# Attention, a Mish MLP and a SoLU MLP on one core: the SoLU MLP's first product computed for pairs of token tiles by a seven-product scheme

## The chip, the cores and the metric

The kernel runs on one core of a Trainium2 chip. The metric is the device time of one execution in microseconds, smaller being better. Engines are named as in the profile: PE (TensorE, matmuls; PEld its weight loads), DVE (VectorE), ACT (ScalarE), POOL (GpSimd), SP (SyncE, which issues the DMAs here).

## The reference

Causal attention over a window of 64 (4 x 8 heads, 576 tokens, head size 64) feeds an MLP with the Mish function (512 to 2048 to 512), and that feeds a second MLP, with SoLU and a LayerNorm (512 to 1024 to 512). There are 2304 tokens.

```python
x = attention(q, k, v)                      # 2304 x 512
h = x @ w_in                                # first MLP, 2048 wide
x = (h * np.tanh(log1p(exp(h)))) @ w_out
h = x @ w_in2                               # second MLP, 1024 wide: the change is here
e = np.exp(h - max(h))
solu = h * (e / (sum(e) + 1e-09))
mu = mean(solu);  var = mean((solu - mu) ** 2)
ln = (solu - mu) / np.sqrt(var + 1e-06) * g_ln
return ln @ w_out2
```

## The kernel before

**Number format.** Every fp32 product is made of three matmul terms: each operand is split in a high part rounded to a short format (`round_12`) and a rest (`rest`), and high x rest, high x high and rest x high are summed in PSUM. The weights arrive as 64-bit numbers; four steps on ACT and DVE (`c_up`, `c_low`, `c_bits`, `c_sign`, lines 350 to 372) turn a piece of them in a staging buffer `st` into fp32, and `c_hi`, `c_lo` split it into a weight buffer (`w1` or `w2` ring, four buffers each). g_ln is multiplied into the last weights in the same split.

**First MLP.** Tokens stand in groups of 512, 512, 512, 384 and 384. An item is one group by one block of 128 hidden units; there are 84. Item i has 12 matmuls into `ps_h` (`pe_m1`, L742), Mish on ACT and DVE, and 12 more into the four output banks `x_0` to `x_3` (`pe_m2`, L776, and `pe_m2l`, L787). Attention (lines 462 to 727) is computed in pieces between the items of the first groups. A group's output is copied out by L812 and L814 and stored to a scratch tensor `x2d`.

**Second MLP.** It goes by tiles of 128 tokens, t = 0 to 17. `b_load` fetches a tile into `xr`; `b_split` (ACT, L855) and `b_rest` (POOL, L860) split it into `xs`; `b_m3` (L870) makes 24 matmuls of 128 x 512 into the two banks of `h2`, turn by turn: four blocks of the contraction by three terms by two halves of the 1024 columns. Then comes a chain of one tile: `b_max` (DVE, L877), `b_exp` with a row sum (ACT, L883), `b_stat` (DVE: product with h in L889, two `bn_stats` in L892, L894 to L899), `b_var` (POOL, L904 and L905, the inverse square root by `pow`), `b_z` (DVE, L910 and L911), eight transposes on PE (`b_tr`, L918), the split of the transposed tile (`b_hi` on ACT, L924; `b_lo` on DVE, L928), 24 matmuls into one bank `po` (`b_m4`, L943), `b_out` (ACT, L950) and the store. `h2` has two buffers, one for even and one for odd tiles.

**Order.** Nothing is ordered by hand. Every piece of work is a `step` with its costs on the engines that may do it, a due time and the steps it has to come after. `Schedule.run` (line 113) takes, again and again, the step that can start first by its own planned costs, and among those that can start within `PATIENCE` the one that is due first. Buffers are rings (`w1=4, w2=4, st=2, ...`): a step that needs a new one waits until the users of the oldest are done. The due times of every stage come from number tables (`MISH_AT`, `ATT_AT`, `PRE_AT`, `B_AT`, `CONV_PRIO`, ...), so one number in a table can move instructions on all engines. In each engine's queue the instructions are then executed in the order that results.

**Where PE has nothing to do** in the first stage, small bf16 matmuls on a zero tile (L516) are put in; 42 of them stand at the start.

Of the kernel before, what the change touches and what calls it, by code (L numbers as in the profile page):

```python
# [24 lines left out]
P = 128  # L25
# [30 lines left out]
B_AT = (9.587, 37.912, -19.559, -30.209, 0.809, 34.651, 64.819, 43.703)

CONV_PRIO = (43.465, 59.161, 15.699, 11.465, 9.993, -9.387)
Q_LEAD = 1.101
V_LEAD = -62.18  # L60
G_AT = 1.058
K0_LATER = -88.806
FIRST_AT = (-161.938, -95.173, -8.712)
W_STEP = 0.88
M4_LATER = -28.799
BESIDE_AT = ((12.83, 25.285), (5.132, 29.901), (-14.786, 53.657), (-18.384, 60.677), (13.158, 1.338))
BESIDE_PE = 15.387
PATIENCE = 0.35
SLACK = 7.152
# [6 lines left out]
N_STAGED = 4  # L76
W1_PIECES = ((0, 1), (1, 1), *((f, 2) for f in range(2, 16, 2)))
# [119 lines left out]
def attention_moe_solu(  # L197
# [81 lines left out]
    tctx = ExitStack()  # L279
    ld_p = tctx.enter_context(tc.tile_pool(name="ld", bufs=LD, side="right"))  # L280
# [541 lines left out]
    with tc.manual_schedule():  # L822
# [8 lines left out]

        def open_b():
            tctx.close()
            B["x"] = ctx.enter_context(tc.tile_pool(name="bx", bufs=2, side="right", reuse_waits="tile"))
            B["s"] = ctx.enter_context(tc.tile_pool(name="bs", bufs=4, side="right", reuse_waits="tile"))
            B["h0"] = ctx.enter_context(tc.tile_pool(name="pb_h0", bufs=1, space=PSUM, side="right", reuse_waits="tile"))
            B["mhalf"] = B["s"].tile([P, 1], F32, name="mhalf", bufs=1)
            nc.vector.memset(B["mhalf"], -0.5)

        def open_b2():  # L840
# [4 lines left out]
            B["h1"] = ctx.enter_context(tc.tile_pool(name="pb_h1", bufs=1, space=PSUM, reuse_waits="tile"))  # L845

        def b_load(t):
            j, o = tile_of[t]
            xr[t] = B["x"].tile([P, KD, P], F32, tag="xr", name="xr", bufs=1)
            nc.sync.dma_start(out=xr[t], in_=x2d[j][:, :, o:o + P])  # L850

        def b_split(t):
            r = xr.pop(t)
            xs[t] = B["x"].tile([P, 2, KD, P], F32R, tag="xs", name="xs", bufs=2)
            nc.scalar.activation(out=xs[t][:, 0], in_=r, func=ACTF.Copy)  # L855
            xr[t] = r

        def b_rest(t):
            r = xr.pop(t)
            nc.gpsimd.tensor_tensor(out=xs[t][:, 1], in0=r, in1=xs[t][:, 0].bitcast(F32), op=ALU.subtract)  # L860

        def b_m3(t):
            h2[t] = B["h" + str(t % 2)].tile([P, 2, 512], F32, tag="h2", name="h2")
            x = xs.pop(t)
            assert all(("w3", c, k) in split_done for c in range(2) for k in range(KD))

            terms = [(k, a, b) for k in range(KD) for a, b in ((0, 1), (0, 0), (1, 0))]
            for idx, (k, a, b) in enumerate(terms):
                for c in range(2):
                    nc.tensor.matmul(  # L870
                        out=h2[t][:, c, :], lhsT=x[:, a, k, :], rhs=wt["w3", c][:, b, k, :],
                        start=(idx == 0), stop=(idx == len(terms) - 1),
                    )

        def b_max(t):
            nm = B["s"].tile([P, 1], F32, tag="nm", name="nm")
            nc.vector.tensor_reduce(out=nm, in_=h2[t], axis=AX.XY, op=ALU.max, negate=True)  # L877
            nrm[t] = nm

        def b_exp(t):  # L880
            y = B["x"].tile([P, 2, 512], F32, tag="y", name="y")
            su = B["s"].tile([P, 1], F32, tag="su", name="su")
            nc.scalar.activation(out=y, in_=h2[t], func=ACTF.Exp, bias=nrm[t], accum_out=su)  # L883
            nrm[t] = y, su

# [371 lines left out]
```

## Time and profile before

| | us |
|---|---|
| median of 3 runs | 705.45 (704.46 to 706.88) |
| profiled execution | 706.97 |
| its span, first to last instruction | 705.1 |
| PE busy | 695.4 (4429 matmuls) |
| DVE busy | 382.0 |
| ACT busy | 312.1 |
| POOL busy | 56.9 |

Busy time is the sum over an engine's instructions. Matmuls are pipelined and overlap in the profile's bars, so one matmul's listed duration is longer than the time that it adds to the span; what one adds is read from the chain of waits, where consecutive matmuls of one line form a piece with its length and count.

### The profile page before, as it was taken

What the parts mean: (1) busy time and instruction counts of PE and PEld (TensorE: products, weight loads), DVE (VectorE), ACT (ScalarE), POOL (GpSimd) and SP (SyncE); (2) the same over time, 40 slices, a digit from 0 to 9 for tenths busy, and PEclk for the clock granted to TensorE, in tenths of its full rate; (3) what the DMA queues carried; (4) which work ended last, traced back from release to release, by engine and by line L of the source; (5) the groups of instructions that cost most, each with busy time, mean ns of one, the idle gap of its engine ahead of it and who ended that gap; (6) DMA issues with size and microseconds to landing.
All of it is one profiled execution on the core that took longest, in us unless ns stands there. A gap on an engine that the chain in (4) does not pass through costs nothing.

```text
span 705.1 us, 10722 instructions
## 1 busy us (share of the span) xinstructions
PE 695.4 (99%) x4429; PEld 597.2 (85%) x4429; DVE 382.0 (54%) x559; ACT 312.1 (44%) x536; POOL 56.9 (8%) x80
## 2 busy tenths in 40 slices
PE   9989999999999999999999999999999999999997
PEld 7779888888888888878899999999888888888886
DVE  4988776775662121656614114666766556565550
ACT  5769977475442222454534325663322222222231
POOL 2111000010000000000001100001122212111000
PEclk9999999999999999999999999999999999999999
DMA  8747355846213030323150105330111111110011
GB/s 288 296 156 293 121 178 179 278 160 219 90 46 106 0 119 31 119 91 120 31 165 1 31 1 165 120 119 32 44 59 46 46 45 46 46 45 31 16 45 46
DMA packets 37856, 71.74 MB, mean 102 GB/s; under 512 B 2864, under 2 KB 15152, under 8 KB 37808
## 3 DMA queue, kind: packets, MB, share of 16 engines
q1 hardware_dynamic: 37808, 71.06, 29.9%
q8 instruction: 35, 0.57, 0.3%
q14 instruction: 13, 0.11, 0.0%
HBM read 59.51 MB, written 11.53 MB: 101 GB/s over the span
## 4 chain that ended last, share of the span: by engine, by line
PE 94%; DVE 3%; DMA 2%; ACT 1%; issue 0%; SPq 0%; ACTq 0%
PE ps_h L742 27%; PE x L776 18%; PE h L870 14%; PE po L943 14%; PE x L787 9%; PE ps_o L696 2%; PE pt L918 2%; PE ps_t L659 2%; PE ps_s L564 2%; PE ps_w L516 1%; DMA st<-w_in 1%; DMA room_kv<-v 1%; PE ps_s L546 1%; DVE w L308 0%; DVE g L308 0%; DVE su L633 0%
## 5 line engine op out<-in xcount | busy, mean ns | idle before, releaser
L742 PE MATMUL ps_h<-xt,w 128*128 128x512 f32 (+2 forms) x1008 | 212.3, 361 | 0.3 <-ACT mc L752 0.2
L742 PEld LDWEIGHTS ps_h<-xt,w 128*128 128x128 f32 x1008 | 178.1, 189 | 22.9 <-issue 1.0
L776 PE MATMUL x<-g,w 128*128 128x512 f32 (+2 forms) x672 | 147.9, 362 | 0.0
L776 PEld LDWEIGHTS x<-g,w 128*128 128x128 f32 x672 | 118.1, 188 | 14.6 <-issue 0.9
L308 DVE SCALAR_TENSOR_TENSOR g<-mc,g 128x512 fp32r<-128x512 f32 (+2 forms) x84 | 53.2, 635 | 117.5 <-ACT g L288 117.0
L870 PE MATMUL h<-w,xs 128*128 128x512 f32 x432 | 104.0, 396 | 0.0
L943 PE MATMUL po<-w,lz 128*128 128x512 f32 x432 | 102.8, 394 | 0.0
L870 PEld LDWEIGHTS h<-w,xs 128*128 128x128 f32 x432 | 80.9, 188 | 19.0
L943 PEld LDWEIGHTS po<-w,lz 128*128 128x128 f32 x432 | 80.0, 188 | 16.3
L288 ACT ACTIVATE g<-mc 128x512 fp32r<-128x512 f32 (+2 forms) x70 | 39.8, 572 | 97.9 <-PE x L787 97.5
L787 PE MATMUL x<-g,w 128*128 128x512 f32 (+2 forms) x336 | 81.2, 363 | 0.0
L752 ACT ACTIVATE mc<-ps_h 128x512 f32<-128x512 f32 (+2 forms) x84 | 44.6, 535 | 78.1 <-PE ps_h L742 64.3
L787 PEld LDWEIGHTS x<-g,w 128*128 128x128 f32 x336 | 59.1, 188 | 7.1 <-issue 0.5
L924 ACT ACTIVATE lz<-pt 128x512 fp32r<-128x512 f32 x36 | 19.6, 596 | 63.2 <-PE po L943 49.5
L877 DVE TENSOR_REDUCE nm<-h 128x1 f32<-128x1024 f32 x18 | 22.0, 1224 | 45.8 <-PE h L870 45.8
L647 POOL TENSOR_TENSOR s<-s,rs 128x1024 f32<-128x1024 f32 x7 | 13.5, 1934 | 348.8 <-DVE rs L641 342.8
L368 DVE SCALAR_TENSOR_TENSOR st<-st 128x1024 uint32<-128x1024 uint32 x22 | 26.9, 1224 | 25.5 <-ACT st L360 25.5
L855 ACT ACTIVATE xs<-xr 128x512 fp32r<-128x512 f32 x18 | 11.4, 632 | 59.7 <-issue 32.2
L860 POOL TENSOR_TENSOR xs<-xr,xs 128x512 fp32r<-128x512 f32 x18 | 23.3, 1293 | 167.6 <-ACT xs L855 167.6
L889 DVE TENSOR_TENSOR y<-h,y 128x1024 f32<-128x1024 f32 x18 | 22.0, 1223 | 14.5 <-ACT y L883 14.5
L928 DVE TENSOR_TENSOR lz<-pt,lz 128x512 fp32r<-128x512 f32 x36 | 23.3, 686 | 12.2 <-ACT lz L924 11.0
L353 ACT ACTIVATE st<-st 128x1024 f32<-128x1024 f32 x22 | 25.3, 1149 | 9.5 <-DMA st<-w_in 6.4
(102 smaller groups left out, 651.7 us busy)
## 6 DMA issues: line engine op xcount, KB each, us to landing
qk<-qk SPq DMA_DIRECT2D x32, 512.0 KB, 5.0
st<-w_out SPq DMA_DIRECT2D x12, 1024.0 KB, 5.0
st<-w_in SPq DMA_DIRECT2D x10, 1024.0 KB, 5.7
v<-v SPq DMA_DIRECT2D x32, 256.0 KB, 3.4
xr<-x2d SPq DMA_DIRECT2D x18, 256.0 KB, 3.1
out<-o SPq DMA_DIRECT2D x18, 256.0 KB, 2.0
x2d<-xs SPq DMA_DIRECT2D x12, 256.0 KB, 2.9
part<-xs SPq DMA_DIRECT2D x8, 256.0 KB, 3.2
```

The lines of the kernel that those rows point to most:

```text
L288: nc.scalar.activation(out=hi, in_=x, func=ACTF.Copy, scale=1.0 if g is None else g)
L308: nc.vector.scalar_tensor_tensor(out=lo, in0=x, scalar=1.0 if g is None else g, in1=hi.bitcast(F32), op0=ALU.mult, op1=ALU.subtract)
L353: nc.scalar.activation(out=w, in_=w, func=ACTF.Copy, scale=2.0**-112)
L368: nc.vector.scalar_tensor_tensor(out=lw, in0=uw, scalar=3, in1=lw, op0=ALU.logical_shift_left, op1=ALU.bitwise_or)
L742: nc.tensor.matmul(out=ps[:, :n], lhsT=w[:, a, k, fs], rhs=x[:, b, k, a0:a1], start=(idx == 0), stop=(idx == len(terms) - 1),)
L752: nc.scalar.activation(out=c[:, :n], in_=ht.pop(i)[:, :n], func=ACTF.Mish)
L776: nc.tensor.matmul(out=acc[j][m][:, a0:a1], lhsT=w[:, a, f % 4, m * P:(m + 1) * P], rhs=g[:, 0, :n], start=(i in opens and a == 0), stop=F ...
L787: nc.tensor.matmul(out=acc[j][m][:, a0:a1], lhsT=w[:, 0, f % 4, m * P:(m + 1) * P], rhs=g[:, 1, :n], start=False, stop=i in closes,)
L860: nc.gpsimd.tensor_tensor(out=xs[t][:, 1], in0=r, in1=xs[t][:, 0].bitcast(F32), op=ALU.subtract)
L870: nc.tensor.matmul(out=h2[t][:, c, :], lhsT=x[:, a, k, :], rhs=wt["w3", c][:, b, k, :], start=(idx == 0), stop=(idx == len(terms) - 1),)
L928: nc.vector.tensor_tensor(out=lt[t][:, 1, fs], in0=pst[t][:, fs], in1=lt[t][:, 0, fs].bitcast(F32), op=ALU.subtract)
L943: nc.tensor.matmul(out=po[t], lhsT=lz[:, a, f, :], rhs=wt["w4", f // 4][:, b, f % 4, :], start=(c == 0 and idx == 0), stop=(c == 2 and idx ...
```

## The change

**The product.** Two tiles of tokens (i = 0, 1 of pair u) form the left operand, cut in halves along the contraction: A11, A12 of the first tile, A21, A22 of the second. w_in2 is cut into four quarters of 256 x 512. In place of eight half-products, seven are computed (`PRODUCTS`; Winograd's form of Strassen's scheme). Left sums: S1 = A21 + A22, S2 = S1 - A11, S3 = A11 - A21, S4 = A12 - S2 (`b_sum`, four DVE operations for a pair). The four sums of the weights (`t_sum`) are made once, and seven weight halves are split and kept. A product is six matmuls of 128 x 512: two blocks of the contraction by three terms. One of the four banks is added to twice and one once, and between two products on one bank its content is copied out to `v_b` (`b_v`): four copies per pair. `b_c` adds bank and copy into `h_b` in SBUF, four times per pair, with one VectorE instruction that also gives the row maximum (`tensor_tensor_reduce`).

**The chain.** `b_max` now takes the greater of two numbers. `b_y` multiplies h by the exponentials and sums the rows in one `tensor_tensor_reduce`; the sum of squares of the centred values is made by ACT (`b_sq`, a Square with accumulator); `bn_stats` is gone. `b_pow` on POOL has the two instructions that `b_var` had. `b_rest` on POOL is gone: the rests of `xs` are made by DVE now (`b_lo_a`, `b_lo_s`), the high parts by ACT (`b_hi_a`, `b_hi_s`) or DVE.

**Buffers.** h is in SBUF in four buffers. PSUM holds one bank each for the four sums, one for transposes, two for `po`. `xs` of odd pairs is in the `w1` ring's fourth buffer, `v_b` in the `w2` ring; the weight sums and the left sums of pairs 0 and 1 in a buffer of the first MLP's operand (`raw`, tag `xt`). Three weight pieces (`EXTRA`) are staged in a pool `e` of two buffers that is opened where attention's buffers were.

**Tables.** All tables of due times have other numbers.

```diff
-B_AT = (9.587, 37.912, -19.559, -30.209, 0.809, 34.651, 64.819, 43.703)
+B_AT = (-7.004, 14.468, -32.863, -57.388, -27.681, -6.194, 50.167, 71.418)
+P_AT = (-6.653, -154.42, 27.689, 37.086, -6.1, 36.23)
+EXTRA = (19, 20, 23)
...
+    T_OF = {1: (("st", 1), ("st", 0)), 2: (("st", 3), ("t", 1)), 3: (("st", 3), ("st", 1)), 4: (("st", 2), ("t", 2))}
+    def t_sum(e, i):
...
+        eng.tensor_tensor(out=w3_t[i], in0=a, in1=b, op=ALU.subtract)
...
-            h2[t] = B["h" + str(t % 2)].tile([P, 2, 512], F32, tag="h2", name="h2")
-            terms = [(k, a, b) for k in range(KD) for a, b in ((0, 1), (0, 0), (1, 0))]
-            for idx, (k, a, b) in enumerate(terms):
-                for c in range(2):
-                    nc.tensor.matmul(
-                        out=h2[t][:, c, :], lhsT=x[:, a, k, :], rhs=wt["w3", c][:, b, k, :],
...
+            for i, a, b, op in (
+                (0, a21, a22, ALU.add), (1, s[:, 0], a11, ALU.subtract), (2, a11, a21, ALU.subtract),
+                (3, a12, s[:, 1], ALU.subtract),
+            ):
+                nc.vector.tensor_tensor(out=s[:, i], in0=a, in1=b, op=op)
...
+        PRODUCTS = ((0, 0, 0, True), (3, 3, 1, True), (1, 1, 2, True), (4, 4, 0, False), (6, 2, 1, False),
+                    (2, 6, 3, True), (5, 5, 0, False))
+        def b_p(u, i):
+            ix, iw, bank, first = PRODUCTS[i]
...
+            terms = [(k, a, w) for k in range(2) for a, w in ((0, wlo), (0, whi), (1, whi))]
+            for n, (k, a, w) in enumerate(terms):
+                nc.tensor.matmul(
+                    out=ps, lhsT=x[:, a, ix, k, :], rhs=w[:, k, :], start=first and n == 0, stop=n == len(terms) - 1,
+                    skip_group_check=not first,
+                )
+        def b_v(e, u, n, bank):
+            copy(e, B["v"][:, n], banks[u, bank])
+        def b_c(u, i, c):
...
+            nc.vector.tensor_tensor_reduce(
+                out=hs[t][:, c], in0=B["v"][:, 3] if bank is None else banks[u, bank], in1=B["v"][:, v], scale=1.0,
+                scalar=-3.0e38, op0=ALU.add, op1=ALU.max, accum_out=mx[t][:, c:c + 1],
+            )
...
-            nc.vector.tensor_reduce(out=nm, in_=h2[t], axis=AX.XY, op=ALU.max, negate=True)
...
-            nc.vector.tensor_tensor(out=y, in0=h2.pop(t), in1=y, op=ALU.mult)
-            for c in range(2):
-                nc.vector.bn_stats(out=st[:, c, :], in_=y[:, c, :])
...
+            nc.vector.tensor_tensor_reduce(
+                out=y, in0=y, in1=e, scale=1.0, scalar=0.0, op0=ALU.mult, op1=ALU.add, accum_out=st[:, :1]
+            )
...
+        def b_sq(t):
+            nc.scalar.activation(out=e, in_=y, func=ACTF.Square, bias=st[:, 1:2], accum_out=st[:, 3:4])
...
+                if not first:
+                    after = after + [vs_[bank][-1]]
```

**The order that results.** PE's queue has 378 matmuls of the second MLP's first product, 432 before; the counts of all its other matmuls stay, but for two of the zero fillers. DVE's queue has 664 rows, 535 before; ACT's 517, 470 before; POOL's 65, 79 before.

PE where the first MLP ends, before: the last matmuls of tile 0's `b_m3` and what stands behind them (`w_3887`, `w_4038` are w_in2, `w_1726` the first MLP's second weights).

```order
L870 MATMUL h_4331<-w_3887,xs 128x512
L870 MATMUL h_4331<-w_4038,xs 128x512
L776 MATMUL x_0_3940<-g,w_1726 128x384 [waits Activation_49]
L776 MATMUL x_0_3940<-g,w_1726 128x384
L776 MATMUL x_1_3941<-g,w_1726 128x384 x2
L776 MATMUL x_2_3942<-g,w_1726 128x384 x2
L776 MATMUL x_3_3943<-g,w_1726 128x384 x2
L787 MATMUL x_0_3940<-g,w_1726 128x384 [waits DVE_49]
```

PE at the same place with the change: the last rows of the first MLP, then products of pair 0 (`w_3912`, `w_4036`, `w_4182` hold weight halves).

```order
L833 MATMUL x_3_3923<-g,w_1545 128x384
L957 MATMUL pb<-w_3912,xs 128x512 [waits PE_49]
L957 MATMUL pb<-w_3912,xs 128x512 x5
L957 MATMUL pb<-w_4036,xs 128x512 [waits Activation_49]
L957 MATMUL pb<-w_4036,xs 128x512
L957 MATMUL pb<-w_4036,xs 128x512 [waits DVE_49]
L957 MATMUL pb<-w_4036,xs 128x512 x3
L957 MATMUL pb<-w_4182,xs 128x512 [waits Activation_49]
L957 MATMUL pb<-w_4182,xs 128x512 x5
```

Before, four sets of the first MLP's second product stood behind the first tile's matmuls; with the change all of them stand ahead of the second MLP's first product, and the products of pairs 0 and 1, 84 matmuls, follow without anything between.

ACT from there on, before: the Exp of tile 0, which is the first one of the second MLP, with its table load.

```order
L883 ACT_TABLE_LOAD [waits DMAHW7_49]
L883 ACTIVATE y,su<-h_4331,nm 128x1024 [waits DVE_49]
L812 ACTIVATE xs<-x_0_3940 128x384 [waits PE_49]
L812 ACTIVATE xs<-x_2_3942 128x384 [waits DMAHW7_49,PE_49]
L812 ACTIVATE xs<-x_3_3943 128x384 [waits DMAHW0_49,PE_49]
L924 ACTIVATE lz<-pt 128x512 [waits PE_49,Activation_49]
```

ACT at the same place with the change: `xs` of pair 2 is split, bank copies of pair 1, the table load and Exp of tile 0, the Square of tile 0, and the splits of tile 0's transposes (`lz`).

```order
L296 ACTIVATE xs<-xr 128x256 [waits DMAHW4_49,PE_49]
L308 ACTIVATE v_b<-pb 128x512 [waits DVE_49,PE_49,Activation_49]
L989 ACT_TABLE_LOAD
L989 ACTIVATE e,su<-h_b,nm 128x1024 [waits DVE_49]
L296 ACTIVATE xs<-s_b 128x1024
L308 ACTIVATE v_b<-pb 128x512 [waits DVE_49,PE_49,Activation_49]
L308 ACTIVATE v_b<-pb 128x512 [waits PE_49]
L1008 ACTIVATE e,st<-h_b,st 128x1024 [waits DVE_49,Activation_49]
L989 ACTIVATE e,su<-h_b,nm 128x1024 [waits DVE_49]
L308 ACTIVATE v_b<-pb 128x512 [waits PE_49]
L1046 ACTIVATE lz<-pt 128x512 [waits PE_49]
```

Between the Exp of a tile and the split of its transposes stand now bank copies of a later pair, a split of 1024 columns and a Square.

PE in the settled stretch, before: from the transposes of one tile to the matmuls of `b_m3` of a later one.

```order
L918 MATMUL pt<-ident,y 128x128 [waits DVE_49,PE_49]
L918 MATMUL pt<-ident,y 128x128 x7
L943 MATMUL po<-w_4177,lz 128x512 [waits Activation_49]
L943 MATMUL po<-w_4177,lz 128x512 x7
L943 MATMUL po<-w_4309,lz 128x512 x8
L943 MATMUL po<-w_4177,lz 128x512 x4
L943 MATMUL po<-w_4309,lz 128x512 x4
```

PE in the settled stretch with the change: from one tile's transposes through products of a pair to `b_m4` (L1065).

```order
L1040 MATMUL pt<-ident,h_b 128x128 [waits DVE_49,PE_49]
L1040 MATMUL pt<-ident,h_b 128x128 x7
L957 MATMUL pb<-w_4036,xs_w 128x512 x6
L957 MATMUL pb<-w_4182,xs_w 128x512 [waits Activation_49]
L957 MATMUL pb<-w_4182,xs_w 128x512 x5
L957 MATMUL pb<-w_4036,xs_w 128x512 [waits Activation_49]
L957 MATMUL pb<-w_4036,xs_w 128x512 x5
L957 MATMUL pb<-w_4351,xs_w 128x512 x6
L957 MATMUL pb<-w_4182,xs_w 128x512 [waits Activation_49]
L957 MATMUL pb<-w_4182,xs_w 128x512 x5
L1065 MATMUL po<-w_4058,lz 128x512 x8
```

A block of 24 matmuls without a wait has become products of six, of which three in a pair wait for ACT's copy of their bank; the transposes of the pair's other tile stand among them, and two tiles' `b_m4` follow.

## Rows read from the trace of the kernel before

**Rows 1.** The page, its parts 1 and 2: busy us (share) of engines; granted clock.
```profile
PE 695.4 (99%) x4429; PEld 597.2 (85%) x4429; DVE 382.0 (54%) x559; ACT 312.1 (44%) x536; POOL 56.9 (8%) x80
...
PEclk9999999999999999999999999999999999999999
```

**Rows 2.** Busy us of each engine in stretches (from:to us, length), clock, DMA share, GB/s.
```profile
core 0: us, PE busy (x) PEld busy (x) DVE busy (x) ACT busy (x) POOL busy (x), PEclk, DMA share, GB/s
0.00:50.00 50.00, 44.23 (x495) 37.94 (x496) 37.35 (x61) 31.45 (x81) 9.86 (x21) 0.97 0.69 243
50.00:100.00 50.00, 50.00 (x483) 43.38 (x482) 40.69 (x52) 45.45 (x99) 3.80 (x2) 1.00 0.59 206
400.00:450.00 50.00, 49.80 (x287) 49.42 (x286) 17.23 (x23) 21.14 (x34) 0.00 (x0) 1.00 0.27 87
...
574.00:598.00 24.00, 24.00 (x114) 19.79 (x113) 13.38 (x25) 6.83 (x12) 4.17 (x6) 1.00 0.14 44
```

**Rows 3.** PE's own waits, whole span: for whom, us in total, times, longest.
```profile
PE ps_s L564 <- DVE xt L718: 1.9, 1, 1.9
...
PE ps_h L742 <- ACT mc L752: 0.2, 1, 0.2
```

**Rows 4.** The chain of waits: start us, length us, engine, tile, line, matmuls in the piece.
```profile
477.77 5.60 PE h L870 x24
...
524.08 1.84 PE po L943 x8
...
546.32 5.48 PE po L943 x24
...
688.60 12.74 PE po L943 x56
```

**Rows 5.** The page, part 5: weight loads of `b_m3`, busy us, mean ns.
```profile
L870 PEld LDWEIGHTS h<-w,xs 128*128 128x128 f32 x432 | 80.9, 188 | 19.0
```

**Rows 6.** VectorE by line and form: count, busy us, mean ns, idle before.
```profile
L928 DVE TENSOR_TENSOR lz<-pt,lz 128x512 fp32r<-128x512 f32 x36 | 23.3, 686 | 12.2 <-ACT lz L924 11.0
...
L889 DVE TENSOR_TENSOR y<-h,y 128x1024 f32<-128x1024 f32 x18 | 22.0, 1223 | 14.5 <-ACT y L883 14.5
L308 DVE SCALAR_TENSOR_TENSOR w<-st,w 128x1024 fp32r<-128x1024 f32 x18 | 21.9, 1224 | 5.4 <-ACT w L288 5.2
...
L911 DVE TENSOR_SCALAR y<-y,mv,c 128x1024 f32<-128x1024 f32 x18 | 14.6, 813 | 0.7
...
L897 DVE RECIPROCAL r<-r 128x1 f32<-128x1 f32 x18 | 3.0, 164 | 0.6
...
L718 DVE TENSOR_TENSOR xt<-ps_o,xt 128x256 fp32r<-128x256 f32 x4 | 1.5, 406 | 0.0
```

**Rows 7.** ScalarE by line and form, the same columns.
```profile
L883 ACT ACTIVATE y<-h,nm 128x1024 f32<-128x1024 f32 x18 | 20.1, 1117 | 20.4 <-PE pt L918 14.3 <-DVE nm L877 6.1
L924 ACT ACTIVATE lz<-pt 128x512 fp32r<-128x512 f32 x36 | 19.6, 596 | 63.2 <-PE po L943 49.5 <-PE pt L918 8.3 <-issue 5.3
...
L950 ACT ACTIVATE o<-po 128x512 f32<-128x512 f32 x18 | 10.9, 604 | 12.8 <-issue 7.7 <-PE po L943 5.1
...
L288 ACT ACTIVATE w<-st 128x1024 fp32r<-128x1024 f32 x7 | 7.9, 1138 | 3.0 <-PE ps_h L742 1.8 <-DVE st L374 1.2
...
L883 ACT ACTIVATION_READ_ACCUMULATOR y<-h,nm 128x1 f32 x18 | 3.5, 193 | 0.0
...
L883 ACT ACT_TABLE_LOAD x1 | 1.3, 1283 | 0.0
```

**Rows 8.** POOL by line and form, the same columns.
```profile
L860 POOL TENSOR_TENSOR xs<-xr,xs 128x512 fp32r<-128x512 f32 x18 | 23.3, 1293 | 167.6 <-ACT xs L855 167.6
L905 POOL TENSOR_TENSOR va<-va,mhalf 128x1 f32<-128x1 f32 x18 | 10.2, 566 | 1.5
```

**Rows 9.** The timeline at the end: start us, length us, engine, line, count [idle before].
```profile
688.36 12.97 PE L943 MATMUL po<-w,lz 128*128 128x512 f32 x56
...
701.41 0.60 ACT L950 ACTIVATE o<-po 128x512 f32<-128x512 f32 x1 [4.84 <-PE po L943]
```

More of the change, by code (lines that the diff above doesn't have):

```diff
@@ L76 @@
 N_STAGED = 4
+W_AT = -57.813
+EXTRA = (19, 20, 23)
 W1_PIECES = ((0, 1), (1, 1), *((f, 2) for f in range(2, 16, 2)))
@@ L850, in b_load @@
[L850 to L862, printed above, removed]
[L863 to L873 removed]
+            if i == 0:
+                xr[u] = B["x"].tile([P, 2, KD, P], F32, tag="xr", name="xr")
@@ new lines, in b_hi_s, with b_lo_s @@
+        def b_hi_s(e, u):
+            round_12(e, ops[u][:, 0, 3:], sums[u])
+        def b_lo_s(e, u):
+            rest(e, ops[u][:, 1, 3:], sums[u], ops[u][:, 0, 3:])
+        PRODUCTS = ((0, 0, 0, True), (3, 3, 1, True), (1, 1, 2, True), (4, 4, 0, False), (6, 2, 1, False),
+                    (2, 6, 3, True), (5, 5, 0, False))
+        def b_p(u, i):
+            ix, iw, bank, first = PRODUCTS[i]
+            if first:
+                banks[u, bank] = B["p0" if bank < 2 else "p1"].tile([P, 512], F32, tag=f"p{bank}", name="pb")
+            ps, x = banks[u, bank], ops[u]
+            whi, wlo = w3_halves(iw)
+            terms = [(k, a, w) for k in range(2) for a, w in ((0, wlo), (0, whi), (1, whi))]
[4 more added lines that the diff above has]
+                )
@@ L970, in attention_moe_solu @@
         first_ld = []
+        e_bufs = []
+        oe = step(dict(none=0.0), 0, open_e)
         def convert(p):
@@ L975, in convert @@
             key = nm, p["c"]
-            fresh = key not in whole
+            fresh = nm != "w3" and key not in whole
             if fresh:
@@ L999, in convert, with w3_split, t_step, convert_w3 @@
             for i in range(k):
-                split_of[nm, p["c"] if nm == "w3" else 0, f + i] = lo
+                split_of[nm, 0, f + i] = lo
+        raw = Buf("xt")
+        w3_s, w3_buf, w3_done = {}, {}, []
+        def w3_split(i, u, hi_fn, lo_fn, arg, after, st):
+            key = i // 2
+            new = []
+            if key not in w3_buf:
+                w3_buf[key] = Buf("w1" if i < 6 else "w2")
+                new = [w3_buf[key]]
+            o = CONV_PRIO
+            hi = step(COSTS["t_hi"], u + o[4], hi_fn, arg, after=after + first_hi.get(("w3", key), []), new=new, uses=st)
+            first_hi.setdefault(("w3", key), [hi])
+            w3_done.append(step(COSTS["t_lo"], u + o[5], lo_fn, arg, after=[hi], uses=st))
+        def t_step(i, u, after, st):
+            t = step(COSTS["t"], u + T_AT[0], t_sum, i, after=after + list(w3_t1), new=[raw] if i == 1 else [], uses=[raw] + st)
+            if i == 1:
+                w3_t1.append(t)
+            w3_split(2 + i, u + T_AT[1], t_hi, t_lo, i, [t], [raw])
+            return t
+        w3_t1 = []
+        def convert_w3(n, u, sign, st):
+            p = next(p for p in pieces if p.get("w3") == n)
+            note = step(dict(none=0.0), u, c_note, p, after=[sign], uses=[st])
+            w3_s[n] = note, st
+            if n != 1:
+                w3_split((0, None, 1, 2)[n], u, c_hi, c_lo, p, [note], [st])
+            if n == 1:
+                w3_s["t1"] = t_step(1, u, [note, w3_s[0][0]], [st, w3_s[0][1]])
+            elif n == 3:
+                w3_s["t2"] = t_step(2, u, [note, w3_s["t1"]], [st])
+                t_step(3, u, [note, w3_s["t1"]], [st, w3_s[1][1]])
+            elif n == 2:
+                t_step(4, u, [note, w3_s["t2"]], [st])
+        def c_note(p):
+            w3_st[p["w3"]] = p["wf"]
         for p in pieces:
@@ L1163, in attention_moe_solu @@
         attention_done = list(pv_of.values()) + list(x_of.values())
-        ob = step(dict(none=0.0), 0, open_b, after=attention_done)
+        oe.after += attention_done
+        ob = step(dict(none=0.0), 0, open_b, after=attention_done + [x for b in e_bufs for x in b["users"]])
         ob2 = step(
```

286 lines of the change are left out of this document (213 added, 73 removed).

## Prediction

> **What bounds the kernel now.** I read the page's busy shares first. PE is busy 695.4 of 705.1 us, DVE 382.0, and the granted clock is full in all 40 slices [rows 1]. A share of 99% is a mean, so I looked next at stretches: the first 50 us have 44.23 us of PE, the next 50.00 of 50, and a stretch of two tiles of the second MLP has 24.00 of 24.00, with DVE at 13.38, ACT at 6.83 and POOL at 4.17 [rows 2]. PE's own waits say the same: they lie in the first 50 us, and after that one of 0.2 us is left [rows 3]. So from 50 us to the last matmul the end moves by exactly what PE's queue gets shorter or has to wait. How long a matmul keeps the queue is read from the chain of waits. 24 matmuls of the second MLP's first product make 5.60 us, which is 0.2333 each; 24 of its second product, which go into one bank, make 5.48 (0.2283), and a piece of 56 makes 12.74 (0.2275) [rows 4]. Weight loads, 188 ns each, hide under that [rows 5].
>
> **What is removed.** 432 matmuls at 0.2333 are 100.8 us. 378 come back, in 63 products of six into one bank. I take the one-bank price: 378 x 0.2275 = 86.0, plus a start of about 0.02 for each product, which is what a piece of eight has over eight times 0.2275 (1.84 against 1.82) [rows 4]: 87.3, or 1.385 a product. Saved: 13.5. Ends: 54 x 0.2333 = 12.6, if alternating banks was not what made 5.60, and 100.8 - 86.0 = 14.8.
> The Trainium skill, "TensorE: Matmul & The Clock Gate", section "Wait — 56ns, not 53.3ns?", gives 215.7 ns from start to start for 512 columns with a warm array. No piece in this trace is so short, and by the page 54 fewer matmuls would save 11.6; the trace decides.
>
> **What is added off PE, in the settled stretch.** A pair now takes PE 7 x 1.385, plus 2 x 5.48 for the second product, plus 16 transposes. A tile's period was 12.0 [rows 2], of which 5.60 and 5.48 are matmuls, so eight transposes take 0.9. Together 9.7 + 11.0 + 1.8 = 22.4 us, 24.0 before.
> VectorE, per pair: four sums of 256 columns at 0.406 (1.6); rests of 512, 256 and 1024 columns (0.69 + 0.41 + 1.22 = 2.3); four additions from a bank of 512 columns at 0.686 and two of 1024 at 1.223, each with a short second instruction, which I put at 0.1 (5.2 + 0.6); two scalings at 0.813 (1.6); four rests of the transposes at 0.686 (2.7); twelve single-column steps, at most 0.164 each (I take 1.7) [rows 6]. Sum 15.7 of 22.4. I have no row of a `tensor_tensor_reduce` here; I take the plain two-operand rows as nearest, with as many elements in and out, which is the lower bound too, as it reads and writes no fewer; twice that is the upper one, for an instruction that passes over its data again to add up.
> ACT, per pair: high parts of 512, 256 and 1024 columns (0.6 + 0.4 + 1.14), four bank copies at 0.6, two Exp and two Squares at 1.117 + 0.193, four splits at 0.596, two outputs at 0.604 [rows 7]: 13.4 of 22.4. POOL loses 18 x 1.293 and keeps its `pow` steps [rows 8]. All three have room, so what counts is whether a step is late.
> One place repeats: three products of a pair wait for ACT's copy of their bank. In the settled order one product (1.385) lies between two on the same bank, and a copy takes about 0.6 with 0.1 to 0.2 to signal. These three copies stand in ACT's queue ahead of the next Exp, so 0.6 us is left, and I charge nothing. If an Exp or Square (1.31) stood ahead of one, 1.31 + 0.6 + 0.1 = 2.0 against 1.385 would cost PE 0.6. The tile chains are covered with over 10 us, since h has four buffers in SBUF.
>
> **Where I do expect a wait: the passage from MLP to MLP.** Before, four sets of the first MLP's matmuls stood behind tile 0's products and covered its chain. Now nothing does. Let T be the first product's start, where the first MLP's matmuls end. Pair 0's products end at T+9.7, pair 1's fifth would start at T+15.2. It needs the copy of a bank that ACT makes after the table load (1.28), Exp of tile 0 (1.31) and a split of 1024 columns (1.14) [rows 7]. ACT's preceding copy, of pair 1's first product, ends 0.6 after that product: T+11.7. So 11.7 + 1.28 + 1.31 + 1.14 + 0.6 = 16.0, with signals 16.3. Wait 1.1. The products then end at T+20.5. Tile 0's Exp ends at T+14.3. Behind it come DVE's product and small steps (1.7), the Square behind a copy (1.3 + 0.6), small steps around `pow` (1.3), about 0.8 of a rest of 1024 columns that DVE does in between, and the scaling (0.8) [rows 6 to 8]: 6.5, with signals its transposes start at T+21.0. Wait 0.5. The second product follows directly on the transposes, so ACT's first split (0.6, and signals) is seen in full: 0.85. Sum 2.5. Bounds: 0.5, if ACT finds more room than my queue, and 5, if the products with the new instruction take twice as long.
> The weights of the second MLP need ten more operations of 1024 columns (four sums, three high parts, three rests), 1.14 to 1.22 each [rows 6, 7], 12 us on DVE and ACT. They lie beside PE from 400 us on, where DVE has 17.23 and ACT 21.14 of 50 [rows 2], and PE's cover is the queue of the first MLP. I charge nothing; if one Mish step slips behind two of them, PE waits 1 to 2.
> The zero fillers, two fewer, are 0.2 less. The order of attention has been renewed, and in the first 50 us PE has 5.8 us idle [rows 2]: this can go either way, 1.5 each side, and I take 0. The end stays: after the last product six sets of the second product follow, against a piece of 56 before, then one output copy of 0.6 [rows 9].
>
> **Sum.** The profiled execution took 706.97 us, 1.87 of it outside its span; it is 1.5 above the median of 705.45. 706.97 - 13.5 + 2.5 - 0.2 = 695.8 for that execution, a change of -11.2, so 694.3 against the median. All good ends at once (14.8 saved, 0.5 waited, 1.5 from the front) give 689.5, all bad ones 699.2; as they hardly fall together, the forecast's own range is 691 to 698.5.
>
> **The rivals.**
> *A, PE waits for bank copies in every pair.* For it: three dependent copies a pair, ACT's queue holds Exp and Square for other tiles, and one late Square holds the copies behind it. Against: ACT is idle 9 of 22.4 us and the three copies stand together. One or two waits of 0.6 in each of 9 pairs are 5.4 to 10.8: 699.7 to 705.1, middle 702.
> *B, the renewed order of the front and the weights' path.* Longer: one late weight piece or Mish step, 3 to 5 us, 697.5 to 699.5, since three weight pieces now wait for the end of attention before they can be fetched. Shorter: up to half of the 5.8 idle us goes, 691.5.
> *C, VectorE becomes the bound, the slower side.* The two `tensor_tensor_reduce` forms take 5.2 us a pair at plain price [rows 6]. At double price VectorE has 20.9 of 22.4, and the sum grows only at the passage, to about 696.5. At triple price it has 26.1: 3.7 us over PE in each of 9 pairs, 33 in all, 727. It is slower than before from an excess of 11.2/9 = 1.2 a pair, which is 2.5 times the plain price. Against: every two-operand fp32 row, with a bank or with two SBUF operands, lies on one line, about 0.13 us and 1.06 per 1000 columns (256: 0.406, 512: 0.686, 1024: 1.223) [rows 6].
> The Trainium skill, "Vector Engine (DVE) Microarchitecture Reference", section "Points that are easy to get wrong", says that the two-operand form with an accumulator runs at half throughput where both sources are in SBUF and not bf16. Of the six such instructions of a pair three would double (one of 512 columns, two of 1024), which is 3.1 us more; 18.8 of 22.4 is still below PE, and tile 0's product in the passage is 1.2 longer: 695.5. No row here shows such an instruction: the nearest without an accumulator, two SBUF operands of 1024, is at full rate, 1224 ns [rows 6].
> *D, that fewer matmuls do not run.* The order has 378 against 432, so I give it nothing.
>
> **How the numbers follow.** Forecast (694.3, within 691 to 698.5) 0.68; A 0.13; B longer 0.08, shorter 0.04; C beyond its break-even 0.05; rest 0.02. For 8 in 10 I take the forecast, a third of A and all of B: 690.5 to 701. A difference of 0.3% (2.1 us) is about what a measurement can tell from none. Slower is C and a little of the rest, 0.05; same, 703.3 to 707.6, is the end of A and of the rest, 0.06; faster 0.89.
>
> **What would show it.** In the changed profile: the chain's product pieces of six at 1.37 to 1.40; PE busy about 13.5 less; PE waits on `pb`, `pt` and `po` in the 25 us after the last matmul of the first MLP, and none on the copies later. Rival A shows as waits of `pb` on ACT spread over all pairs; C as `ISA` rows well above 0.69 and 1.22 and a DVE near its full share; B in the busy time before 480 us. The forecast is wrong if a product takes 1.40 or more, or if the passage costs over 5 us.

## The result and the profile after

The changed kernel takes 699.19 us (median of 4 runs, 698.40 to 700.07), the kernel before 704.97 (median of 4 runs, one more than in the table of before, 704.46 to 706.88): a ratio of 0.9913, 95% interval 0.9890 to 0.9937. By the ratio that is 6.1 us less (4.4 to 7.8), by the medians 5.8, where 11.2 were forecast. The time lies in the stated range (690.5 to 701), outside the forecast's own one (691 to 698.5). So some 5 us of the expected gain are missing, and the question is where they went.

The page of the changed kernel, its first lines (busy us of each engine, share of the span, instructions):

```profile
span 697.2 us, 10836 instructions
...
PE 680.7 (98%) x4373; PEld 584.7 (84%) x4373; DVE 398.3 (57%) x689; ACT 363.7 (52%) x612; POOL 49.1 (7%) x68
```

PE is 14.7 us less busy than in [rows 1], and the span is only 7.9 shorter. So PE stands idle for longer. Busy time by stretches of the changed kernel (stretch, length, then PE, PEld, DVE, ACT, POOL busy, clock, DMA share, GB/s):

```profile
0.00:50.00 50.00, 43.95 (x528) 37.52 (x529) 37.54 (x62) 32.01 (x84) 11.91 (x23) 1.00 0.71 251
50.00:100.00 50.00, 45.13 (x429) 39.07 (x430) 35.49 (x47) 47.47 (x95) 5.69 (x3) 1.00 0.56 197
...
550.00:572.30 22.30, 22.30 (x108) 18.41 (x107) 18.23 (x51) 13.65 (x24) 1.47 (x4) 1.00 0.15 47
```

Against [rows 2], the stretch from 50 to 100 us has gone from 50.00 to 45.13 us of PE: 4.87 us of idle PE, in attention, 400 us ahead of the changed products. ACT is busy 47.47 of 50 there, 45.45 before. The settled stretch of the second MLP has no idle PE. PE's waits in the changed kernel (for whom, us in total, times, longest):

```profile
PE ps_s L610 <- DVE xt L764: 3.1, 2, 2.5
PE ps_o L742 <- ACT s L308: 2.0, 1, 2.0
...
PE x L822 <- ACT g L296: 1.0, 1, 1.0
PE ps_t L705 <- POOL s L693: 1.0, 1, 1.0
...
PE po L1065 <- ACT lz L1046: 0.7, 1, 0.7
PE pb L957 <- ACT v_b L308: 0.6, 1, 0.6
...
PE pt L1040 <- DVE h_b L1033: 0.4, 1, 0.4
```

The first four lines belong to attention and the first MLP. The first of them was 1.9 in the kernel before [rows 3], the other three are new. The last three, 1.76 us by the timeline, are the passage into the second MLP.

What ACT does in the bad stretch shows in its timeline (start us, length us, engine, line, operation):

```profile
57.15 1.28 ACT L641 ACT_TABLE_LOAD   x1
...
60.01 0.57 ACT L308 ACTIVATE xt<-ps_o 128x512 fp32r<-128x512 f32 x1
60.59 1.28 ACT L798 ACT_TABLE_LOAD   x1
61.89 0.39 ACT L798 ACTIVATE mc<-ps_h 128x256 f32<-128x256 f32 x1
62.29 1.28 ACT L641 ACT_TABLE_LOAD   x1
...
65.26 1.28 ACT L798 ACT_TABLE_LOAD   x1
```

L641 is attention's Exp, L798 the Mish of the first MLP. For one Mish of 0.39 us ACT loads two tables, 2.57 us. From 50 to 100 us it loads 7 tables in the kernel before (count | busy us, mean ns | idle before):

```profile
L752 ACT ACT_TABLE_LOAD x4 | 5.1, 1283 | 0.1
...
L595 ACT ACT_TABLE_LOAD x3 | 3.8, 1283 | 0.1
```

and 11 in the changed kernel:

```profile
L798 ACT ACT_TABLE_LOAD x6 | 7.7, 1283 | 0.5 <-PE ps_h L788 0.5
L641 ACT ACT_TABLE_LOAD x5 | 6.4, 1283 | 0.1
```

The four more are 4 x 1.283 = 5.1 us on an engine that had 4.5 us left. Nine of the eleven stand whole on the chain of work that ended last, which in this stretch of the kernel before is PE's matmuls alone.

### The profile page after: what moved, and what is told of

Its sections match the earlier page's. It is cut to its first block, busy times and chain, and to the rows that moved or that the text cites. A ratio compares the mean times of both kernels' runs of the same rounds, so it can differ in the third digit from the quotient of the medians.

```text
span 697.2 us, 10836 instructions
## 1 busy us (share of the span) xinstructions
PE 680.7 (98%) x4373; PEld 584.7 (84%) x4373; DVE 398.3 (57%) x689; ACT 363.7 (52%) x612; POOL 49.1 (7%) x68
## 4 chain that ended last, share of the span: by engine, by line
PE 88%; ACT 6%; DVE 2%; DMA 1%; issue 1%; SPq 0%; POOL 0%; ACTq 0%; POOLq 0%
PE ps_h L788 26%; PE x L822 18%; PE po L1065 14%; PE pb L957 11%; PE x L833 9%; PE pt L1040 2%; PE ps_s L610 2%; PE ps_o L742 2%; PE ps_t L705 2%; DMA st<-w_out 1%; PE ps_w L562 1%; ACT s L641 1%; ACT L641 1%; ACT L798 1%; ACT st L362 1%
## 5 line engine op out<-in xcount | busy, mean ns | idle before, releaser
L798 ACT ACTIVATE mc<-ps_h 128x512 f32<-128x512 f32 (+2 forms) x84 | 44.8, 536 | 133.9 <-PE ps_h L788 132.2
L1065 PE MATMUL po<-w,lz 128*128 128x512 f32 x432 | 100.5, 390 | 0.7 <-ACT lz L1046 0.7
L1065 PEld LDWEIGHTS po<-w,lz 128*128 128x128 f32 x432 | 80.7, 188 | 17.6 <-ACT lz L1046 0.9
L957 PE MATMUL pb<-w,xs 128*128 128x512 f32 x210 | 50.9, 398 | 0.0
L296 ACT ACTIVATE g<-mc 128x512 fp32r<-128x512 f32 (+2 forms) x61 | 35.0, 576 | 28.0 <-PE x L833 26.8
L957 PEld LDWEIGHTS pb<-w,xs 128*128 128x128 f32 x210 | 38.9, 188 | 8.9
L693 POOL TENSOR_TENSOR s<-s,rs 128x1024 f32<-128x1024 f32 x11 | 20.9, 1898 | 317.5 <-DVE rs L687 306.5
L957 PE MATMUL pb<-w,xs_w 128*128 128x512 f32 x168 | 40.4, 394 | 0.6 <-ACT v_b L308 0.6
L308 ACT ACTIVATE v_b<-pb 128x512 f32<-128x512 f32 x34 | 20.2, 597 | 34.5 <-PE pb L957 34.5
L957 PEld LDWEIGHTS pb<-w,xs_w 128*128 128x128 f32 x168 | 31.0, 188 | 7.3 <-ACT v_b L308 1.1
L1020 POOL TENSOR_SCALAR va<-va 128x1 f32<-128x1 f32 x18 | 9.8, 546 | 289.1 <-DVE va L1013 289.1
L1072 ACT ACTIVATE o<-po 128x512 f32<-128x512 f32 x18 | 10.8, 601 | 35.7 <-PE po L1065 22.4
```

The costliest lines, as they stand in the source:

```text
L296: nc.scalar.activation(out=hi, in_=x, func=ACTF.Copy, scale=1.0 if g is None else g)
L308: nc.scalar.activation(out=out, in_=x, func=ACTF.Copy)
L693: eng.tensor_tensor(out=s, in0=s, in1=rs.to_broadcast(list(s.shape)), op=ALU.mult)
L798: nc.scalar.activation(out=c[:, :n], in_=ht.pop(i)[:, :n], func=ACTF.Mish)
L957: nc.tensor.matmul(out=ps, lhsT=x[:, a, ix, k, :], rhs=w[:, k, :], start=first and n == 0, stop=n == len(terms) - 1, skip_group_check=not ...
L1065: nc.tensor.matmul(out=po[t], lhsT=lz[:, a, f, :], rhs=wt["w4", f // 4][:, b, f % 4, :], start=(c == 0 and idx == 0), stop=(c == 2 and idx ...
```

## Experiments

**Theory F:** the seven products bring what was forecast, and the renewed numbers lose 5 us in attention by four more table loads. **Theory P:** the products bring less than 11 us, and the front (all that stands ahead of the second MLP's first product) is scatter.

### The two parts of the change, each alone

`old_tables`: the changed kernel with the numbers of before.

```diff
-MISH_AT = (-8.867, 3.546, 47.632, -64.249, -4.772)
+MISH_AT = (-4.796, 28.112, 34.41, -45.879, 4.491)
...
-SLACK = 26.697
+SLACK = 7.152
```

> The changed kernel with every due-time number of before; the products, the chain and the buffers stay as changed. PE's, ACT's and VectorE's queues are then those of before, row for row, up to about the 75th item of the first MLP. Theory F (the missing 5 us were lost in the stretch from 50 to 100 us, where the renewed numbers make ACT change between Exp and Mish tables 11 times instead of 7): PE's busy time in 50 to 100 us is back at 50.0 and the time is about 5 us below the changed kernel, 694, plus what the second MLP loses by numbers not made for it (0 to 4). Theory P (the seven products bring less than 11 us, the front is only scatter): 699 or more.

Measured: 694.50 us, ratio 0.9856 (0.9832 to 0.9880). PE is busy 50.00 of 50 us from 50 to 100 us again.

`new_tables_old_product`: the kernel before with the numbers of the changed one (the same diff the other way round).

> The kernel before with every number of the changed one that it has too; the second MLP has its 432 matmuls. All queues are those of the changed kernel up to the second MLP. Theory F: 45 of 50 us of PE in the stretch from 50 to 100 us, and 705 + 5 to 6 = 710 to 711. Theory P: PE loses nothing there by the numbers alone, 705.

Measured: 710.42 us, ratio 1.0074 (1.0052 to 1.0096): slower, by the numbers alone, with no product changed. Its stretch and its chain (start us, length us, matmuls of the piece):

```profile
50.00:100.00 50.00, 45.11 (x442) 38.93 (x436) 36.02 (x47) 46.96 (x94) 5.69 (x3) 1.00 0.55 196
```

```profile
490.12 16.80 PE h L870 x72
...
694.41 10.92 PE po L943 x48
```

PE loses here what it loses in the changed kernel, 4.9 us. And since the front is the same, this is the kernel to set the changed one against: its second MLP takes 705.33 - 490.12 = 215.2 us from the first product to the last matmul. The changed kernel's chain:

```profile
489.57 11.20 PE pb L957 x48
...
518.69 9.80 PE pb L957 x42
...
537.07 4.09 PE pb L957 x18
...
682.47 10.92 PE po L1065 x48
```

That is 693.39 - 489.57 = 203.8 us, 11.4 less. By the medians, 710.42 to 699.19 is 11.2, the forecast's number; by the ratios, 1.0074 against 0.9913, it is 11.4, give or take 2.3. Theory P falls.

### The table loads by themselves

`four_loads_fewer`:

```diff
-        nc.scalar.activation(out=c[:, :n], in_=ht.pop(i)[:, :n], func=ACTF.Mish)
+        nc.scalar.activation(out=c[:, :n], in_=ht.pop(i)[:, :n], func=ACTF.Exp if i in (6, 8) else ACTF.Mish)
```

> The changed kernel with Exp in place of Mish in items 6 and 8 of the first MLP, each of which stands alone between Exps of attention: part of the Mish is not computed. That takes away four table loads (11 to 7 in the stretch from 50 to 100 us) and nothing else; all other rows of all queues stay. Theory F: 4 x 1.283 = 5.1 us less on ACT, which bounds that stretch; PE's 4.9 idle us there go, 694 to 695. If the loads lie beside other waits: 0 to 2 us.

Measured: 693.65 us, ratio 0.9839 (0.9817 to 0.9862), 5.5 below the changed kernel. The stretch:

```profile
50.00:100.00 50.00, 49.46 (x475) 42.99 (x464) 40.51 (x52) 44.84 (x93) 5.69 (x3) 1.00 0.58 204
```

All but 0.5 us of the idle PE is gone, with four instructions of ACT taken out and all else in its place; the two Exps take as long as the two Mish did (0.37 and 0.59 us against 0.39 and 0.60). This separates the loads from everything else that the numbers moved: they are the cause. They cost their full length: the idle time that ACT had in this stretch took up none of it. The Trainium skill, "ScalarE: Activation LUTs", section "What ACT_TABLE_LOAD costs", gives 2.66 us for every switch to a different set, about 1.283 for the load and 1.38 for a drain. This trace does not agree: the activation ahead of the load of 60.59 ends at 60.58, the load ends at 61.87, and the Mish behind it starts at 61.89, so that the load alone is the price. (The time given back can't tell this: PE had no more than 4.9 idle us to give.)

### Both together

`joined` takes the numbers of before for attention, the first MLP and its weights and for the scheduler's `PATIENCE` and `SLACK`, and those of the change for the second MLP, its weights and the last 20 items of the first MLP.

```diff
-MISH_AT = (-8.867, 3.546, 47.632, -64.249, -4.772)
+MISH_AT = (-4.796, 28.112, 34.41, -45.879, 4.491)
...
+M2_AT = 5.714; LATE_MISH = (-8.867, 3.546, 47.632, -64.249, -4.772)
...
-            o = [pos[i] + x for x in MISH_AT]
+            o = [pos[i] + x for x in (MISH_AT if i < 64 else LATE_MISH)]
```

> The changed kernel with the numbers of before for attention, first MLP and its weights, and the changed numbers for the second MLP, its weights and the last 20 items of the first MLP. Queues as before up to the 64th item, then nearly as in the changed kernel. Theory F: no idle PE from 50 to 100 us and the short second MLP together, 693.5 to 695. Theory P: 699.

Measured: 692.87 us, ratio 0.9826 (0.9806 to 0.9846), faster than either kernel: 6.3 below the changed one. From 50 to 100 us PE is busy 50.00, and the second MLP takes 687.94 - 484.22 = 203.7.

### What a product costs: the place of its stationary operand

The forecast priced a matmul of a product at 0.2275 and a start of 0.02, because they go to one bank and those before changed banks. The chain above says otherwise. 42 matmuls, the seven products of an even pair (stationary operand, `lhsT` in the code: `xs`), make 9.80 us, 0.2333 each; 18 of an odd pair (`xs_w`) make 4.09, 0.2272. In both, the six matmuls of a product go to one bank. By the addresses in the built program, which the profile does not show, `xs` starts at 480 modulo 512 bytes in a partition, in the kernel before too, and `xs_w`, `xt` and `lz` at 160.

`xs_moved` and `before_xs_moved` put an unused tile ahead:

```diff
-            ectx.close()
+            ectx.close(); B["pad"] = ctx.enter_context(tc.tile_pool(name="padp", bufs=1, side="right")).tile([P, 80], F32, tag="pad", name="pad"); nc.gpsimd.memset(B["pad"], 0.0)
```

> The changed kernel with an unused tile of 320 bytes per partition ahead of the pool of even pairs' xs, so that xs starts at 160 modulo 512 as xs_w of the odd pairs does (480 before; 32 bytes past a multiple of 64 in both); all queues stay. In the changed kernel's chain, products from xs take 0.2333 per matmul and products from xs_w 0.2275, though both write one bank. Theory S (the place of the stationary operand in SBUF modulo 512 sets it): 210 matmuls x 0.0058 = 1.2 us less, pieces of 42 at 9.56 instead of 9.80. Theory B (bank turns, as the prediction had it, or the region at the top of SBUF): pieces and time stay.

> The kernel before with 320 unused bytes ahead of the pool of xr, xs and y, so that xs starts at 160 modulo 512; the 24 matmuls of a tile still change banks with each matmul, and all queues stay. Theory S: pieces of 24 at 5.46 to 5.48 instead of 5.60, 432 x 0.0058 = 2.5 us less, 702. Theory B (the turns of the banks cost it): 5.60 as before and 704.4.

Measured: `xs_moved` 696.92 us, ratio 0.9894 (0.9876 to 0.9912); its piece of an even pair:

```profile
516.81 9.54 PE pb L957 x42
```

9.54 instead of 9.80: 0.2271 each. Its second MLP takes 690.54 - 487.89 = 202.65 us, 1.2 less than the changed kernel's, as expected. The times can't tell this alone: the median is 2.3 lower, by the ratios it is 1.3, and the intervals of the two ratios overlap; what is over 1.2 lies in the front, where all queues are the same, and so is scatter. `before_xs_moved` 701.34 us, ratio 0.9952 (0.9936 to 0.9967), with banks changing at each matmul as before:

```profile
489.40 5.49 PE h L870 x24
...
654.41 5.45 PE h L870 x24
```

5.45 to 5.49 instead of the 5.60 of [rows 4]. So the turns of the banks cost nothing, and the place cost the kernel before 18 x 0.14 = 2.5 us by its pieces, 3.4 (2.3 to 4.5) by the times.

`shift_64` moved every buffer that PE reads in these products:

```diff
-    g_sb = const.tile([P, NF2], F32, name="g_sb")
+    g_sb = const.tile([P, NF2], F32, name="g_sb"); pad_l = const.tile([P, 8], F32, name="pad_l"); nc.gpsimd.memset(pad_l, 0.0)
...
-            ectx.close()
+            ectx.close(); B["pad"] = ctx.enter_context(tc.tile_pool(name="padp", bufs=1, side="right")).tile([P, 8], F32, tag="pad", name="pad"); nc.gpsimd.memset(B["pad"], 0.0)
```

> The changed kernel with 32 unused bytes per partition ahead of the weight buffers and 32 ahead of xs: every weight buffer, xs_w, xt and lz then starts at 192 modulo 512 and xs at 448, all multiples of 64, where the changed kernel has them 32 past one; all queues stay. If operands 32 bytes off a multiple of 64 cost something, all 3,900 matmuls get shorter: at 0.2275 to 0.2233, for instance, 8 to 10 us. If the step is somewhere else, xs at 448 or nothing at all changes: within 1.5 us of 699.

Measured: 698.72 us, ratio 0.9915 (0.9888 to 0.9942). A piece from `xs`, now at 448:

```profile
518.65 9.57 PE pb L957 x42
```

The other pieces of the second MLP stay within 0.04 us (`po` 5.46 and 10.91). So being off a multiple of 64 costs nothing that shows here.

`xs_at_352` (32 in place of 80 in the diff above):

> The changed kernel with 128 unused bytes ahead of the pool of xs: xs starts at 352 modulo 512, which is 96 modulo 128 as 480 is. Read from the chain's pieces of products from xs, not from the time. If the step comes with 96 modulo 128: 42 matmuls make 9.80 us, 0.2333 each. If it comes with the last 32 bytes of a block of 512 or 256 alone: 9.55, 0.2275, as at 160 and 448.

Measured in its one profile:

```profile
519.66 9.63 PE pb L957 x42
```

0.2293 each. That is between the two, so neither of the two readings holds. At 160 and 448 a matmul of such a piece takes 0.227 to 0.228, at 352 0.229, at 480 0.233. The four places lie within 320 bytes of each other, so the region of the memory is not what counts; the rule behind it stays open, as does the part that the moving operand's place may have.

### The passage between the MLPs

`copy_on_dve`:

```diff
-    "x2": {"act": 0.5, "dve": 0.68},
+    "x2": {"act": 0.5, "dve": 0.68}, "x2d": {"dve": 0.68},
...
-                    cp = step(COSTS["x2"], a + P_AT[4], b_v, u, n, bank, after=[q, ov] + v_last.get(n, []), uses=[bk[bank]])
+                    cp = step(COSTS["x2d"] if (u, i) == (1, 1) else COSTS["x2"], a + P_AT[4], b_v, u, n, bank, after=[q, ov] + v_last.get(n, []), uses=[bk[bank]])
```

> The changed kernel with one of the 36 bank copies, that of pair 1's second product, made by VectorE and not by ACT; other rows stay in order but for this one. In the changed kernel PE waits 0.64 us for it, then 0.43 for tile 0's transposes and 0.69 for their split. Prediction's theory (the copy stands behind table load, Exp and split on ACT): the 0.64 goes. Whether the time falls by it: tile 0's chain ends at most 0.3 earlier, as ACT is rid of 0.6 ahead of the Square, so the wait for the transposes should grow by about as much; net 0 to 0.4 us.

Measured: 700.03 us, ratio 0.9935 (0.9917 to 0.9952); the wait grew from 0.64:

```profile
PE pb L957 <- DVE v_b L310: 1.6, 1, 1.6
```

A miss. PE's wait for the transposes went instead, so that the three waits of the passage add up to 2.3 us where they were 1.76. VectorE's queue had the copy behind tile 0's product `b_y`, which itself waits for the Exp behind the table load. VectorE was idle from 502.4 to 504.3 us with the bank ready, and could not take the copy out of order. Moving the copy to a free engine did not free it from the same wait.

`joined_xs_moved` (the edits of `joined` and `xs_moved`) and `joined_early_load`, which adds to it:

```diff
-            m1_of[i], m2_of[i] = m1, m2
+            m1_of[i], m2_of[i] = m1, m2; act_of[i] = c
...
+        step(dict(act=1.45), -1000.0, lambda: nc.scalar.activation(out=B["pad"][:, 1:2], in_=B["pad"][:, :1], func=ACTF.Exp), after=[ob, act_of[NI - 1]])
```

> The joined kernel (front numbers of before, second MLP's of the change) with xs moved by 320 bytes as in xs_moved; queues as in joined. The place of xs costs 0.0058 on 210 matmuls, 1.2 us, wherever the front is: 692.9 - 1.2 = 691.7. If xs_moved was faster by the scatter of its front alone: 692.9.

> joined_xs_moved with one more ACT instruction, an Exp of one element right behind the first MLP's last Mish, so that the table load comes there, about 20 us ahead of tile 0's Exp; all other rows stay. Prediction's theory of the passage (the load of 1.28 us stands ahead of the copy for which PE waits 0.64 and of tile 0's chain for which it waits 0.43 more): both waits go, 1.1 us less than joined_xs_moved, and the 0.69 for the split of the transposes stays. If the chain is held by VectorE's order instead: 0 to 0.6 less.

Measured: `joined_xs_moved` 692.51 us (5 runs), ratio 0.9815 (0.9799 to 0.9830). By time it can't be told from `joined`; in the traces its second MLP takes 202.45 us against 203.72, the 1.27 expected. `joined_early_load` 691.45 us, ratio 0.9809 (0.9794 to 0.9825); the times don't tell the two apart, and in the traces its second MLP is 0.4 shorter (202.05). Its PE timeline at the passage:

```profile
493.92 9.68 PE L957 MATMUL pb<-w,xs_w 128*128 128x512 f32 x42
504.51 1.09 PE L1040 MATMUL pt<-ident,h_b 128*128 128x128 f32 x8 [0.91 <-DVE h_b L1033]
506.29 5.76 PE L1065 MATMUL po<-w,lz 128*128 128x512 f32 x24 [0.69 <-ACT lz L1046]
```

The wait for the copy is gone, as the theory said. But the wait for the transposes went from 0.43 to 0.91, where it should have gone too. ACT's queue has a copy of pair 1's fourth product ahead of tile 0's Square, and that copy waits for PE; the Square starts at 500.05. So the second MLP got 0.4 us shorter where 1.1 were expected, and most of the rest came back as the next wait. This kernel is the fastest of all, 13.6 us (1.9%) below the kernel before.

### VectorE's room

`adds_twice`:

```diff
-            nc.vector.tensor_tensor_reduce(
-                out=hs[t][:, c], in0=B["v"][:, 3] if bank is None else banks[u, bank], in1=B["v"][:, v], scale=1.0,
+            for _ in range(2):
+                nc.vector.tensor_tensor_reduce(
+                    out=hs[t][:, c], in0=B["v"][:, 3] if bank is None else banks[u, bank], in1=B["v"][:, v], scale=1.0,
```

> The changed kernel with each of its four additions of bank and copy per pair made twice, one after the other, with the same result: 36 more instructions of 0.69 and 36 short ones of 0.08 on VectorE, 3.1 us per pair, which is as much as the page's halved throughput would add. If VectorE has the room that the prediction gives it (15.7 of 22.4): 0 to 1.5 us more, in the passage alone. Rival C (VectorE near its bound): up to 9 x 3.1 = 28 us more.

Measured: 701.94 us, ratio 0.9952 (0.9934 to 0.9969): 2.75 more than the changed kernel, for 28 us more on VectorE. PE's waits for transposes grew from 0.4 us in one place to 1.4 in three:

```profile
PE pt L1041 <- DVE h_b L1034: 1.4, 3, 1.0
```

Busy time by stretches, first of the changed kernel, then of this one:

```profile
500.00:550.00 50.00, 48.24 (x230) 39.33 (x229) 38.67 (x103) 32.83 (x56) 6.73 (x12) 1.00 0.14 43
```

```profile
500.00:550.00 50.00, 47.39 (x224) 38.12 (x223) 46.08 (x127) 32.16 (x55) 6.26 (x10) 1.00 0.14 43
550.00:600.00 50.00, 49.80 (x235) 40.71 (x234) 45.32 (x124) 29.19 (x50) 6.21 (x12) 1.00 0.13 43
600.00:650.00 50.00, 49.94 (x239) 41.29 (x238) 36.05 (x97) 26.04 (x47) 6.65 (x11) 1.00 0.11 37
```

In the 50 us from the passage on VectorE is nearly full (46.08) and PE loses 2.61, 0.85 more than the changed kernel in the same stretch; in the next 50 VectorE is still at 45.32, and from 600 us on it has room. The whole second MLP takes 206.0 us against 203.8, 2.2 more. The other 0.9 us of the two profiles lies ahead of the first product (490.51 against 489.57), where the queues are the same, and so is scatter. So the loss is above my bound of 1.5 (2.2 by the traces, 2.75 by the medians), but far from the 28 us of rival C. I had asked for VectorE's mean load and not for its load while two pairs come in at once. Of the 2.2, PE's longer waits make 0.95; what makes the rest, I did not settle.

## Why the prediction was right, and where it was wrong

**What bounds the kernel:** right but for one stretch. Every gain and loss above is PE's queue or its waits. But "from 50 us to the last matmul" PE was the bound only in the order of before; with the renewed one the chain of work from 57 to 90 us runs through ACT.

**The products:** the sum was right, its reason wrong. 210 matmuls at 0.2333 and 168 at 0.2275 are 87.2 us; the forecast had 87.3. The lower price of one bank, on which it rested, does not exist, and neither does the start of 0.02 per product; the place of `xs` does, and even pairs kept the dear one. The two errors cancelled, which is luck. The prediction's own sign of being wrong, a product of 1.40 or more, stands at its limit: a product of an even pair takes 9.80 / 7 = 1.40, one of an odd pair 1.36.

**The settled stretch:** right. PE 22.30 of 22.30 us in a pair against 22.4 worked out, ACT 13.65 against 13.4. VectorE has 18.23 in the stretch shown, more than the 15.7 worked out, and less than that later; from 489.5 to 693.5 us it is 128.0, 14.2 a pair. No wait on a copy after the passage, so rival A did not come. The new instruction costs what the plain rows said (VectorE by line and form, 550 to 690 us; count, busy us, mean ns, idle before):

```profile
L996 DVE CUSTOM_DVE_ANT_0 h_b<-h_b,e 128x1024 f32<-128x1024 f32 x12 | 14.7, 1221 | 5.6 <-ACT e L989 5.6
L972 DVE CUSTOM_DVE_ANT_0 h_b<-pb,v_b 128x512 f32<-128x512 f32 x18 | 12.2, 684 | 14.8 <-PE pb L957 12.6 <-ACT v_b L308 2.2
...
L972 DVE CUSTOM_DVE_ANT_0 h_b<-v_b 128x512 f32<-128x512 f32 x6 | 4.1, 688 | 0.0
```

684 ns from a bank and 688 from two SBUF operands, 1221 for 1024 columns, as [rows 6] has for plain operations; the second instruction takes 83 ns. The Trainium skill's rule of half throughput ("Vector Engine (DVE) Microarchitecture Reference", section "Points that are easy to get wrong") is not seen here: both forms with two SBUF operands take as long as plain operations. The instruction that stands here is a custom one, so the rule may speak of another; the plain `SCALAR_TENSOR_TENSOR` with two SBUF operands, its accumulator not in use, has 1224 ns in [rows 6] and so no halved rate either.

**The passage:** right in its place and in what PE waits for. The waits are 0.64, 0.43 and 0.69 where 1.1, 0.5 and 0.85 were worked out, 1.8 instead of 2.5. The first is shorter since neighbouring operations of ACT overlap at their ends (two copies together take 1.06, not 1.2). That the table load stands behind the first wait, `joined_early_load` shows; for the other two no run takes the cause away.

**The front:** here the prediction failed, in one sentence: "The order of attention has been renewed [...]: this can go either way, 1.5 each side, and I take 0." What is missing is 5.1, and the renewed numbers by themselves cost 5.2 us (`new_tables_old_product`, 3.7 to 6.8). Rival B named the right part, the renewed order of the front, and had the right time (697.5 to 699.5, though 3 to 5 us on 694.3 are 697.3 to 699.3) and the right sign, PE's busy time ahead of 480 us (469.1 against 474.0); its cause, a late weight piece or Mish step, was another. That the time lies within the stated range is owed to rival B's share in that range, not to the forecast. What would have given the place and the most that it can cost stood in the two orders and in two rows: ACT's queue has four more table loads, a load takes 1.283 us [rows 7], and ACT had 4.5 us left from 50 to 100 us [rows 2]. That ACT's idle time would take up none of the 5.1 us, only the runs showed. I looked at PE's idle time for what the front could lose, though PE had none there; it was ACT, near its bound, that the numbers touched.

**The sum** for the rest of the kernel, 11.2, is what `new_tables_old_product` against the changed kernel measures (11.2), and within its interval what `joined` brings against the kernel before (0.9826: 12.3, 10.8 to 13.7).

## What to carry to other kernels

When a change renews the numbers that set an order, price the order of every stage, also of those that the change doesn't name: count, engine by engine, the instructions that only the order makes (table loads first) in the stretches where that engine is near full. Measure a change of two parts with each part alone; here the numbers cost 5 us and the products brought 11, and the sum looked like a small gain. A due time tuned for the whole may be split by stage and each stage given the better half, which brought 6 us more.

## What was not expected of the hardware

A 128 x 128 x 512 matmul in this format takes 0.227 to 0.228 or 0.2333 us by where its stationary operand starts in SBUF (160 or 448 against 480 modulo 512 bytes; 0.2293 at 352), whether it changes banks with each matmul (`before_xs_moved`) or with each product. Moving the buffers of `xr`, `xs` and `y` by 320 bytes was worth 0.3 to 0.6% to the kernel before, with one memset more in its queues. A table load held ACT for 1.28 us and nothing more: the Mish of 61.89 starts 0.02 us behind its end, and the Exp of tile 0 likewise (501.46 + 1.28, then 502.75).
